# A shorter way to the first scores, a seventh shared PSUM bank and a new plan for the opening of an attention and MLP kernel

## The chip, the core and the metric

The kernel runs on one core of one Trainium2 chip. A time is the device time of one execution in microseconds (us), and a quoted median is over the runs of one job on one chip. The span that a profile shows is some 1.8 us shorter than the time of the same execution. "Slow" means over 1.5% above the fastest run of the same kernel, and comparisons use the other runs.

The engines are TensorE (PE, its weight loads PEld), VectorE (DVE), ScalarE (ACT), GpSimd (POOL) and SyncE (SP). In this kernel POOL issues the loads. SP issues stores, the DMA transposes and the copies of the attention mask ("mask rows").

## The reference, cut to what matters

Block-sparse attention over 4 batches, 8 heads, 768 tokens and head size 64, followed by a residual MLP: a product over the tokens ("token mixing"), then two feed-forward layers of 512 to 2048 to 512.

```python
scores = scale * np.matmul(q, k.transpose(0, 1, 3, 2))
# mask: neighbouring blocks, first and last blocks, three sampled blocks for each query block
scores = np.where(mask, scores, -1000000000.0)
# ... softmax, times v, heads put side by side: x ...
a1 = alpha1 * x + beta1
tok = np.einsum('ts,bsd->btd', w_tok, a1)
u = x + lam * tok
a2 = alpha2 * u + beta2
ch = np.maximum(a2 @ w_ch1, 0.0) @ w_ch2
return (u + lam * ch).astype(np.float32)
```

The kernel works on 16 pairs of heads. The first six pairs take their mask out of the score product ("single scores"). The later ones are multiplied with a mask tile after the exponential ("paired scores").

## The kernel before: the parts that matter

**The order is a plan made ahead.** Every piece of work is a `Job` with an assumed duration, a priority, what it waits for, and the buffers that it takes and gives back. A list scheduler on the host walks through assumed time. Whenever an engine is free it emits the ready job of the best priority, and where TensorE would idle it emits dummy products (`fill`). The result is a fixed instruction order for every engine. `T0` is the assumed time at which the engines are free behind the hand-written opening.

```python
    T0 = 6600.0
    free_at = dict(NEVER=1e9, NONE=0.0, PE=T0, ACT=T0, DVE=T0, POOL=4800.0, SP=T0)
    slots = dict(
        **{b: 1 for b in BANKS}, cp=1, ops=1, eT=NET, head=NQB, vext=NV, ld=NLD, rel=3,
        # ...
    )
```

All loads of q, k and v go through one ring of `NLD = 6` buffers, and they are issued by one queue in a fixed order. A buffer comes free when VectorE has cast its content into another tile:

```python
        putv[p] = Job("DVE", dve(768, 4, 155), (2 if p == 0 else 3, p, 2), pv_put, [ld[p, "v2"]],
                      take=("vext",), give=("ld",))
```

**PSUM.** Six banks are one tile, `ps6`. The second layer adds up in two tiles of its own, `cp` and `ops`. Since `ps6` is one tile, `bank_order` replaces the ordinary ordering by a finer one: it puts waits only between accesses of the same bank. An earlier access of `ps6` stays a reason to wait if the two instructions also share another tile by name:

```python
        for n in names:                      # the other tiles of this instruction
            for r in shared.get(n, ()):      # earlier ps6 instructions that name the same tile
                if r.engine != ins.engine or ins.engine != mybir.EngineType.PE:
                    real[r.name] = r
            shared.setdefault(n, []).append(ins)
        tc.declare_no_dep(ins, group=psum, keep=list(real.values()), reason="other banks")
```

The first layer's evictions (the copies out of PSUM) write the hidden tile `hts` (16 blocks of 384 columns), block `f` by block `f`, out of `ps6`. The second layer's products read four blocks of `hts` at a time.

**The opening.** Nine wide warm products keep TensorE busy until the first operands are there:

```python
    keep_warm(9, 512)
    # ...
    first_cast(0)
    block_mask()          # ends in a subtraction and multiplication on VectorE
    flatA = transposes(rel0, 0, "b0", range(0, 3))
    flatB = transposes(rel0, 0, "b1", range(3, 6))
    for w in range(2):    # mask product, out of kx[0]
        nc.tensor.matmul(t[0:NBLK, 0:HS], mbb[MB, :], kx[0][MB, ts(w, HS)], start=True, stop=True)
    # ... four copies and two casts out of PSUM ...
    keep_warm(7, P)
```

The softmax here doesn't subtract the row's maximum and nothing guards it: scores larger than these inputs give would overflow.

## Time and profile before

| | before |
|---|---|
| time, median of 3 runs | 310.68 us (310.44 to 310.88) |
| span of the profiled execution | 308.2 us |
| first score product starts | 7.72 us |
| last single exponential starts | 67.9 us |
| first paired scores start | 69.9 us |
| dummy products after 8 us, busy time | 6.85 us |
| ScalarE's waits for single scores, 8 to 62 us | 2.4 us |
| second-layer weight loads issued | 38.4 to 43.3 us |

TensorE is busy from one end to the other, so the time can fall only where it is busy with dummies or waits for the opening.

### The profile page before, as it was taken

What the parts mean: (1) busy time and instruction counts of PE and PEld (TensorE: products, weight loads), DVE (VectorE), ACT (ScalarE), POOL (GpSimd) and SP (SyncE); (2) the same over time, 40 slices, a digit from 0 to 9 for tenths busy, and PEclk for the clock granted to TensorE, in tenths of its full rate; (3) what the DMA queues carried; (4) which work ended last, traced back from release to release, by engine and by line L of the source; (5) the groups of instructions that cost most, each with busy time, mean ns of one, the idle gap of its engine ahead of it and who ended that gap; (6) DMA issues with size and microseconds to landing.
All of it is one profiled execution on the core that took longest, in us unless ns stands there. A gap on an engine that the chain in (4) does not pass through costs nothing.

```text
span 308.2 us, 7605 instructions
## 1 busy us (share of the span) xinstructions
PE 302.7 (98%) x3197; PEld 189.0 (61%) x3197; DVE 207.6 (67%) x434; ACT 206.3 (67%) x272; POOL 53.2 (17%) x91
## 2 busy tenths in 40 slices
PE   7999999999999999999999999999999999999995
PEld 3687788775656557555656557555656665555444
DVE  3699898879979788778759788778768730010111
ACT  4999998988676667577676666577658727428000
POOL 4656532001121121212021121120000000000000
PEclk9999999999999999999999999999999999999999
DMA  6999999993347634874444624983110110010121
GB/s 150 186 258 224 212 203 215 177 146 68 51 101 123 104 62 54 146 121 95 76 93 84 102 62 56 147 107 79 28 37 34 28 28 34 34 70 0 50 89 68
DMA packets 47210, 30.81 MB, mean 100 GB/s; under 512 B 27552, under 2 KB 43080, under 8 KB 47176
## 3 DMA queue, kind: packets, MB, share of 16 engines
q0 software_dynamic: 15984, 15.47, 32.0%
q1 hardware_dynamic: 30940, 14.61, 21.0%
q8 instruction: 25, 0.41, 0.6%
q10 hardware_dynamic: 252, 0.24, 0.2%
q14 instruction: 9, 0.07, 0.1%
HBM read 32.04 MB, written 6.33 MB: 124 GB/s over the span
## 4 chain that ended last, share of the span: by engine, by line
PE 76%; DMA 15%; issue 4%; POOL 3%; DVE 1%; POOLq 0%
PE ps L1026 26%; PE cp L1076 22%; DMA v<-in_v_dram 9%; PE ops L870 8%; PE ps L837 8%; PE ps L947 7%; PE ops L1076 5%; DMA k<-in_k_dram 3%; DMA wtk<-in_moe_w_tok_dram 3%; DMA q2f<-in_q_dram 1%; POOL q L383 1%; POOL k L383 1%; POOL w1b L448 1%; POOL v L383 0%; DVE x_sb L957 0%
## 5 line engine op out<-in xcount | busy, mean ns | idle before, releaser
L789 ACT ACTIVATE eT<-ps 128x1024 f16<-128x1024 f32 x90 | 87.0, 1023 | 29.4 <-PE ps L837 28.6
L1026 PE MATMUL ps<-uT,w1b 128*128 128x384 bf16 (+1 forms) x512 | 92.9, 326 | 0.1
L1039 ACT ACTIVATE hts<-ps,b1t 128x384 bf16<-128x384 f32 x106 | 61.4, 583 | 40.3 <-PE ps L1026 36.4
L1076 PE MATMUL cp<-w2b,hts 128*128 128x512 bf16 (+1 forms) x320 | 77.2, 374 | 0.0
L794 DVE TENSOR_TENSOR eT<-eT,maskT 128x1024 f16<-128x1024 f16 x90 | 60.6, 686 | 12.7 <-ACT eT L789 12.5
L1026 PEld LDWEIGHTS <-w1b 128*128 128x128 bf16 x512 | 46.9, 98 | 30.3 <-ACT eT L789 1.0
L1076 PEld LDWEIGHTS <-hts 128*128 128x128 bf16 x400 | 36.6, 98 | 36.4 <-issue 3.0
L731 ACT ACTIVATE eT<-ps 128x1024 f16<-128x1024 f32 (+1 forms) x55 | 52.4, 1020 | 3.4 <-PE ps L716 3.2
L870 PEld LDWEIGHTS <-eT 128*128 128x128 f16 x720 | 30.9, 97 | 15.7 <-issue 3.8
L947 PE MATMUL ps<-a1p,wtokT 128*128 128x128 bf16 x576 | 36.2, 219 | 0.0
L870 PE MATMUL ops<-vext,eT 128*128 128x65 f16 x720 | 35.8, 193 | 0.0
L947 PEld LDWEIGHTS <-wtokT 128*128 128x128 bf16 x576 | 32.9, 98 | 1.5 <-issue 0.6
L1093 DVE TENSOR_TENSOR ot<-x_sb,cp 128x512 f32<-128x512 f32 (+1 forms) x20 | 13.5, 673 | 28.4 <-PE cp L1076 28.3
L716 PE MATMUL ps<-qx,kx 88*128 88x512 bf16 (+1 forms) x144 | 31.7, 326 | 0.7 <-ACT qx L303 0.7
L381 POOL COPY held<-flag 1x1 bf16<-1x1 bf16 x24 | 10.5, 438 | 123.1 <-DVE flag L401 123.1
L837 PE MATMUL ps<-qx,kx 64*128 64x512 bf16 (+1 forms) x240 | 26.1, 326 | 0.0
L756 PEld LDWEIGHTS <-eT 128*128 128x128 f16 x432 | 18.2, 97 | 4.6 <-DVE x_sb L691 0.6
L756 PE MATMUL ops<-vext,eT 128*128 128x65 f16 x432 | 20.2, 193 | 0.0
L957 DVE TENSOR_TENSOR x_sb<-x_sb,ps 128x384 f32<-128x384 f32 x32 | 17.6, 550 | 3.5 <-PE ps L947 3.1
L691 DVE TENSOR_TENSOR x_sb<-ops,rcp 128x384 f32<-128x384 f32 x32 | 17.8, 558 | 1.1
L1093 DVE TENSOR_TENSOR ot<-x_sb,ops 128x512 f32<-128x512 f32 (+1 forms) x5 | 3.2, 635 | 22.5 <-PE ops L1076 22.5
L1043 DVE TENSOR_SCALAR hts<-ps,b1t 128x384 bf16<-128x384 f32 x22 | 13.6, 618 | 6.8 <-PE ps L1026 5.2
(69 smaller groups left out, 227.2 us busy)
## 6 DMA issues: line engine op xcount, KB each, us to landing
out_dram<-ot SPq DMA_DIRECT2D x23, 256.0 KB
v<-in_v_dram POOLq DMA_DIRECT2D x16, 192.0 KB, 4.4
q<-in_q_dram POOLq DMA_DIRECT2D x15, 192.0 KB, 4.7
k<-in_k_dram POOLq DMA_DIRECT2D x15, 192.0 KB, 3.5
w1b<-in_moe_w_ch_dram POOLq DMA_DIRECT2D x4, 512.0 KB, 9.9
w2b<-in_moe_w_ch_dram POOLq DMA_DIRECT2D x4, 512.0 KB, 15.0
wtk<-in_moe_w_tok_dram POOLq DMA_DIRECT2D x3, 384.0 KB, 9.6
maskT<-mask_rows SPq DMA_DIRECT2D x14, 72.0 KB
```

Of the source, the lines that this page charges most:

```text
L691: nc.vector.tensor_tensor(out=x_sb[:, s0 : s0 + NT, h * D : (h + 1) * D], in0=op[:, :, 0:D], in1=rcp[:].unsqueeze(2).broadcast_to([P, NT, D]),
L716: nc.tensor.matmul(sps[:, f - u * UN : f - u * UN + w], kx[h][0:KC, ts(jt, P)], qx[h][0:KC, c : c + w], start=True, stop=True,)
L731: nc.scalar.activation(eT[:, c], sps[:, c], AF.Exp, bias=EXPB, scale=SCALE)
L756: nc.tensor.matmul(ops[p, a][:, t * VW : t * VW + D + 1], eTs[p, u][:, ts(i - u * GU, P)], vx[:, a, jt, 0 : D + 1], start=(i % HT == 0), s ...
L789: nc.scalar.activation(eT[:], sps[:], AF.Exp, bias=EXPB, scale=SCALE)
L794: nc.vector.tensor_tensor(out=e, in0=e, in1=maskT[:, u, :].unsqueeze(1).broadcast_to([P, 2, 512]), op=ALU.min,)
L837: nc.tensor.matmul(sps[:, a * 512 + lo : a * 512 + lo + w], kx[sl][r, ts(jt, P)], qx[sl][r, c : c + w], start=True, stop=True,)
L870: nc.tensor.matmul(ops[p, a][:, t * VW : t * VW + D + 1], eTs[p, u][:, a * 512 + c * P : a * 512 + (c + 1) * P], vx[:, a, jt, 0 : D + 1], ...
L947: nc.tensor.matmul(tp[:, j, :], wtokT[:, s, ts(3 * g + j, P)], tl["a1p", p][:, s, :], start=(s == 0), stop=(s == NT - 1),)
L1026: nc.tensor.matmul(hp[:, 0:nc_], w1b[:, dk, ts(f, P)], uTs[b][:, dk, hf * HS : hf * HS + nc_], start=(dk == 0), stop=(dk == 3),)
L1039: nc.scalar.activation(hts[kk][:, f, :], hp[:, 0:HS], AF.Relu, bias=b1t[:, f : f + 1], scale=1.0)
L1076: nc.tensor.matmul(cps[kk, mi][:, 0:w], hts[kk][:, nk, ts(m, P)], w2tile[0][:, nk, lo : lo + w], start=(nk == 0), stop=(nk == 15),)
```

## The change

The intent is to bring the first scores earlier and use the time saved: one load for two small tables, the mask product out of `kx[3]` so that a copy need not wait for it, the mask arithmetic moved into the evictions, and a shorter warm stretch. Beyond that, the bank `cp` becomes bank `b6` of `ps6`, so that single products may use it until the second layer starts. Three of the first batch's four transposes go to DMA (`UTN`), token mixing of a batch's last pair goes ahead (`PR`, `TOKP`), `LEAD` (how far the plan lets the scores run ahead of the feed-forward layers) becomes 17, and the planner starts at 5.6 us. The core of the diff:

```diff
-LEAD = 18
+LEADS = (17, 17, 17, 17, 17, 17, 17, 17, 17, 17, 17, 17, 17, 17, 17, 17)
+PR = 0
+UTN = 3
+TOKP = 1
+T0 = 5600.0                     # was 6600.0
...
-    ps6 = ps.tile([P, 6 * 512], FP, name="ps6", tag="ps6", bufs=1)
+    ps6 = ps.tile([P, 7 * 512], FP, name="ps6", tag="ps6", bufs=1)
+    ALL = BANKS + ("b6",)
...
-    keep_warm(9, 512)
+    keep_warm(7, 512)
+    keep_warm(2, P)
...
-            t[0:NBLK, 0:HS], mbb[MB, :], kx[0][MB, ts(w, HS)], start=True, stop=True
+            t[0:NBLK, 0:HS], mbm[MB, :], kx[3][MB, ts(w, HS)], start=True, stop=True
...
+    nc.scalar.activation(
+        qx[0][MB, HS:S], bqs[1][0:NBLK, 0:HS], AF.Identity, bias=-BIG, scale=BIG
+    )
...
-        if b == 0:
+        if b == 0 and n >= UTN:
...
-                take = ((("cp", "ops") + (BANKS if kk == 2 * B - 1 else ()), ("cpsel", kk, mi)),) if r == 0 else ()
+                take = ((("b6", "ops") + (BANKS if kk == 2 * B - 1 else ()), ("cpsel", kk, mi)),) if r == 0 else ()
...
-                        opts = BANKS[:2]
+                        opts = BANKS[:2] if st["ch"] else ("b0", "b1", "b6")
```

## The prediction

> **What bounds the kernel now.** I read the page's busy table and its forty slices first, then the order of time of the first 20 us, then the waits, then the windows of the first 80 us.
>
> ```profile
> PE 302.7 (98%) x3197; PEld 189.0 (61%) x3197; DVE 207.6 (67%) x434; ACT 206.3 (67%) x272; POOL 53.2 (17%) x91
> ...
> PE   7999999999999999999999999999999999999995
> ...
> ACT  4999998988676667577676666577658727428000
> ...
> DMA  6999999993347634874444624983110110010121
> ```
> TensorE (PE) is busy from the second slice to the last; ScalarE (ACT) is full only in the first eight slices, to about 62 us, and the DMA engines are full in the same stretch.
>
> Busy PE is not useful PE, so I counted the work. One product of N columns costs N/2.4 GHz plus about 2.7 ns: the trace's stretch of 64 products of 384 columns takes 10.40 us in the chain, 162.5 ns each. First feed-forward layer 512 x 162.7 ns = 83.3 us; second, 368 x 216 plus 32 x 109 = 83.0; token mixing 576 x 56 = 32.3; transposes 132 x 56 = 7.4; value products 1152 x 30.3 = 34.9; single scores 54 x 0.433 = 23.4; paired scores 90 x 0.25 = 22.5. The sum is 286.8 us. The span is 308.2: 7.7 before the first score, some 3.5 behind the last product, and so about 10 us of lost PE time in between. That is all that the later parts of the change can win.
>
> Where those 10 us lie, the waits and the order of time show:
>
> ```profile
> 7.07 0.55 DVE L302 CAST qx<-ps 24x384 bf16<-24x384 f32 x1
> 7.21 0.47 ACT L303 CAST qx<-ops 24x384 bf16<-24x384 f32 x1
> 7.72 1.03 PE L716 MATMUL ps<-qx,kx 88*128 88x512 bf16 x5 [0.66 <-ACT qx L303]
> 8.14 12.31 ACT L731 ACTIVATE eT<-ps 128x512 f16<-128x512 f32 x14 [0.46 <-PE ps L716]
> ```
> The columns are start, length, engine, line. The first score starts at 7.72 us, right after two casts of the mask, and from then on ACT runs exponentials without a gap. The first six head pairs are ACT's stretch: 54 exponentials of 1.02 us, ending at 68.97. PE's real work is too short to fill it, so the kernel puts in dummy products on the warm tile; after 8 us they keep PE some 4.7 us (starts of one group to the next), and none comes after 60 us. Behind 70 us real products stand back to back and lose only 0.02 to 0.04 us in each us inside the groups of products.
>
> **What the Trainium skill says.** "TensorE: Matmul & The Clock Gate", section "What's actually happening": the array starts at half clock and is released after about 3.4 us of sustained work. The trace agrees: the nine first warm products take 427 ns each from 1.19 us, the transposes at 5.01 still go at 107 ns, the products from 6.5 us are fast. So two shorter warm products are affordable, because the array stays busy. "ScalarE: Activation LUTs", "Table sets": identity is in every table set. The trace has one table load, at 2.60 us; the new identity activation should bring no second one. "DMA: Bandwidth & Descriptors", "Issuing engines are not separate DMA queues": all queues share the same 16 engines. The trace agrees: loads that land in 3.3 us at 75 us take 15.0 us at 53, where the windows put the DMA share over 1. "PSUM", "Specifications": eight banks; six shared ones, one for the second layer (cp) and one for the outputs (ops) are all of them, so the seventh bank is cp renamed, not new room.
>
> **The change part by part.**
>
> *Way to the first scores.* Before, warm products hold PE until 5.01 although both casts were done at 4.40 and the weight load of the first transpose started at 4.58. Seven wide and two narrow ones end at 1.19 + 7 x 0.427 + 2 x 0.107 = 4.39, so the transposes come 0.3 to 0.4 us earlier, ending at about 5.5. The copy of kx at 6.31 then waited for the mask product, only because both touch kx0:
>
> ```profile
> DVE kx L298 <- PE ps L294: 1.2, 1, 1.2
> ```
> With the block pattern read from kx3, that copy starts with the transposes' end, some 0.8 us earlier. The subtraction before the mask product (0.38 us on DVE) goes; it moves into the two evictions, which were there anyway. Then DVE has 0.36 + 0.35 + 0.55 = 1.26 us and ACT 3 x 0.47 = 1.41 us from about 5.5, and the first score comes at about 6.95: 0.75 us earlier. Fusing two small tables into one DMA saves an issue of 0.3 us, but the mask chain (ready at 5.11, used at 5.79) was not last. ACT is gap-free behind it, so I count the 0.75 in full.
>
> *Transposes of the first batch.* For three of its four pairs the PE transposes and copies give way to DMA transposes. That takes 18 products of 56 ns off PE, 1.0 us, and two ACT copies of 0.80 and one DVE copy of 0.56. ACT's stretch gets 1.6 us shorter; PE has 1.0 us less to do in it. At most 0.6 more of dummy work goes.
>
> *Seventh bank, priorities, lead of 17.* The single products before the first layer had two banks, now three; token mixing of each batch's last pair and the VectorE work around it go ahead. The dummies at 57.5 us (0.6) and some at 26 to 31 us (1.3) stand where nothing else could go. I grant 0.3 to 1 us of them. Behind 70 us the order changes, the work doesn't.
>
> Sum: 0.75 + 1.0 + about 1.0 = 2.75 us, if the DMA transposes cost nothing.
>
> **The rivals.**
> 1. *The DMA transposes come late.* The SP queue that issues them is taken by the mask rows:
>
> ```profile
> 46.47 15.78 SPq L556 DMA_DIRECT2D maskT<-mask_rows  x18
> 62.55 1.32 SPq L657 DMA_TRANSPOSE qx<-rel  x1
> 63.98 1.81 SPq L657 DMA_TRANSPOSE kx<-rel  x1
> ```
> The second and third pairs' inputs are ready at 45.6 and 50.3 us, so one or both may queue behind the mask, to 62 us, and then land at some 65. The first layer began at 59.7 and did six groups of 0.65 us, 3.9 us, before 69. Without them ACT's stretch ends earlier too (two evictions of 0.73), but 1 to 2 us of dummy or empty PE time appear, and the transposes for pair six start 2.4 us later. Against it: the schedule is a static plan, and whoever set this surely ordered for it. I take 0.5 us off for it on average, so 2.25 remain.
> 2. *ACT stays the bound but at other places.* Then the 0.75 and the 1.6 us of copies are won on ACT, and PE's 1.0 is eaten by dummies: the time falls by 1.5 to 2.3 us, much the same.
> 3. *The early gain is given back.* PE after 70 us is saturated, and an earlier start only lets it start its work earlier; this is not lost unless loads are late. The loads of pairs one and two land at 10 to 13 us, and ACT had no gap there; if ACT runs 0.75 us ahead, it may meet a wait for the second pair's data (dummies at 8.9 to 12.9 show PE waiting). Then 0.3 to 0.7 is lost again and the whole is about 1.5.
> 4. *A large gain.* Over 2% is 6.2 us, which would need nearly all lost PE time and the start; nothing here does it.
>
> **Range and chances.** 310.68 less 2.25 is 308.4. If all goes well, 3 us or a bit more and perhaps some luck of the new order: 306.2. If the late transposes and a wait at 10 us take all, 310.6. A gain over 2% (below 304.5) I give 0.04; a loss over 2% (above 316.9) 0.01.
>
> **What would show it.** The first score in the order of time: right at 6.7 to 7.1 us, wrong if above 7.4. The copy L298's successor must no longer wait for the mask product. One table load. Dummies after 8 us at 3 to 4.5 us against 4.7. The uT transposes: right if all three lie before 57 us, rival 1 if SP issues any behind the mask rows and the first group of the first layer starts after 62 us. Last single exponential: at about 66.5 us if ACT's savings hold, against 68.97. Stretches after 80 us should be as before, shifted. What would make it wrong: a late SP transpose that starves PE, or a re-ordered middle part that loses or wins more than 1 us by itself.

## More of the kernel before

The load queue of this kernel, of which the prediction does not speak, reads as follows in the order of time (columns: start, length, engine, line, output<-input, count, idle time before and what ended it):

```profile
35.92 0.71 POOL L383 DMA_DIRECT2D v<-in_v_dram  x1 [0.44 <-DVE lam_bcb L516]
38.36 0.76 POOL L456 DMA_DIRECT2D w2b<-in_moe_w_ch_dram  x1 [1.73 <-PE ps L947]
...
42.55 0.74 POOL L456 DMA_DIRECT2D w2b<-in_moe_w_ch_dram  x1 [0.29 <-DMA k<-in_k_dram]
51.35 0.70 POOL L383 DMA_DIRECT2D q<-in_q_dram  x1 [8.06 <-DVE rel L571]
```

The four weight loads go out between 38 and 43 us. The queue then waits 8 us for a buffer, with the large loads already under way.

## The result, and the profile after

The changed kernel takes 321.25 us (320.44 to 321.9, four runs), the kernel before 310.78 in the same job. The ratio is 1.0337 with a 95% interval of 1.0306 to 1.0367. It is 3.4% slower, outside the predicted range on the far side. A ratio here is the mean time of one kernel's fast runs over that of the other's of the same rounds, so it is not quite the ratio of the medians.

| | before | after |
|---|---|---|
| first score product | 7.72 | 6.91 us |
| dummy products after 8 us, busy | 6.85 | 9.85 us |
| ScalarE's waits for single scores, 8 to 62 us | 2.4 | 4.4 us |
| last single exponential starts | 67.9 | 70.0 us |
| first paired scores | 69.9 | 85.9 us |
| PE busy in 70 to 80 us | 10.00 | 5.02 us |

The page after, whose rows answer to those that the prediction shows:

```profile
PE 305.4 (96%) x3190; PEld 189.4 (59%) x3190; DVE 207.0 (65%) x433; ACT 204.6 (64%) x269; POOL 53.1 (17%) x91
...
PE   7999999994899999999999999999999999999995
...
ACT  4999699882487756976657666866767534618100
...
PEclk9999999999799999999999999999999999999999
DMA  6999996999519454545647563537021011020021
```

A hole has come up in PE's tenth slice (72 to 80 us) and in ScalarE's at the same place. In the slices before it the DMA row stays high until 80 us, where the row of before falls to 3 at 69. That hole is 5 us of TensorE's time. It has a second price: PEclk, the clock granted to TensorE, falls to 7 in the slice behind it. The clock records of the trace have half clock from 80.04 to 83.45 us, so the 3.1 us of products after the hole took about 1.5 us longer than at full clock (an estimate from these times). The rest of the loss is nowhere to be seen at this resolution.

The opening itself did what it was meant to. In the order of time of the changed kernel:

```profile
5.22 0.36 DVE L302 COPY kx<-ps 64x384 bf16<-64x384 bf16 x1 [0.29 <-PE ps L288]
...
5.88 0.48 ACT L305 ACTIVATE qx<-ops 24x384 bf16<-24x384 f32 x1
...
6.91 1.02 PE L723 MATMUL ps<-qx,kx 88*128 88x512 bf16 x5 [0.65 <-ACT kx L312]
```

The copy of `kx` now waits for the transposes (L288) and no longer for the mask product. The first score starts 0.81 us earlier. There is one table load, at 2.19 us.

The load queue of the changed kernel, in the order of time:

```profile
37.88 0.72 POOL L393 DMA_DIRECT2D k<-in_k_dram  x1
50.45 0.72 POOL L393 DMA_DIRECT2D v<-in_v_dram  x1 [11.85 <-DVE uT L1014]
51.16 3.04 POOL L466 DMA_DIRECT2D w2b<-in_moe_w_ch_dram  x4
54.19 0.71 POOL L393 DMA_DIRECT2D q<-in_q_dram  x1
```

The queue stands still for 11.85 us waiting for a buffer. All six buffers are then held by loads whose casts have not run. In the kernel before, the cast of pair four's v at 34.99 us freed a buffer for the load of pair six's v, issued at 35.92; here that cast comes at 52.03 us, and the load has to take the buffer that the cast of pair five's q frees at 50.15. (Which load takes which buffer was read from the built programs.) The four large weight loads go out at 51 to 54 us instead of 38 to 43. There they meet the mask rows, which SP issues from 51.22 us for 17.6 us. The q of pair seven, issued at 54.19, lands at 76.9 us, 22.7 us later; q loads of the kernel before in the same stretch took 8.4 (median). What that does to VectorE and TensorE:

```profile
76.90 0.36 DVE L578 COPY rel<-q 128x768 bf16<-128x768 bf16 x1 [5.81 <-DMA q<-in_q_dram]
...
79.66 0.62 DVE L1051 TENSOR_SCALAR hts<-ps,b1t 128x384 bf16<-128x384 f32 x1
...
80.34 2.76 PE L1034 MATMUL ps<-uT,w1b 128*128 128x385 bf16 x8 [5.32 <-DVE hts L1051]
```

VectorE waits 5.81 us for q. The eviction of a first-layer bank (L1051) stands behind that in VectorE's order, and TensorE waits 5.32 us for the bank. VectorE kept to its program order here: TensorE's last group before the wait had ended at 75.0 us, so the eviction's bank had been full for over 4 us, and still the eviction started only at 79.66, behind the copy and the work that follows it.

### The profile page after: what moved, and what is told of

The parts are those of the page before. It is cut to its first block, busy times and chain, and to the rows that moved or that the text cites. A ratio compares the mean times of both kernels' runs of the same rounds, so it can differ in the third digit from the quotient of the medians.

```text
span 318.9 us, 7605 instructions
## 1 busy us (share of the span) xinstructions
PE 305.4 (96%) x3190; PEld 189.4 (59%) x3190; DVE 207.0 (65%) x433; ACT 204.6 (64%) x269; POOL 53.1 (17%) x91
## 4 chain that ended last, share of the span: by engine, by line
PE 74%; DMA 13%; issue 6%; ACT 3%; POOL 1%; DVE 1%; SPq 0%; POOLq 0%; ACTq 0%
PE ps L1034 23%; PE ps L1084 22%; PE ops L877 7%; DMA k<-in_k_dram 7%; PE ps L955 7%; PE ps L844 7%; PE ops L1084 5%; DMA v<-in_v_dram 3%; DMA q<-in_q_dram 2%; PE ps L723 2%; ACT eT L796 2%; ACT hts L1047 1%; DMA identb<-ident_c 1%; PE ops L763 1%; PE ps L246 1%
## 5 line engine op out<-in xcount | busy, mean ns | idle before, releaser
L1034 PE MATMUL ps<-uT,w1b 128*128 128x384 bf16 (+1 forms) x512 | 94.3, 329 | 5.3 <-DVE hts L1051 5.3
L1047 ACT ACTIVATE hts<-ps,b1t 128x384 bf16<-128x384 f32 x103 | 59.4, 582 | 47.1 <-PE ps L1034 35.7
L1084 PE MATMUL ps<-w2b,hts 128*128 128x512 bf16 (+1 forms) x320 | 77.1, 375 | 1.1 <-ACT hts L1047 1.1
L1084 PEld LDWEIGHTS <-hts 128*128 128x128 bf16 x400 | 36.8, 98 | 38.2 <-issue 4.4
L877 PEld LDWEIGHTS <-eT 128*128 128x128 f16 x720 | 30.7, 97 | 14.6 <-issue 2.8
L877 PE MATMUL ops<-vext,eT 128*128 128x65 f16 x720 | 35.5, 193 | 0.0
L1101 DVE TENSOR_TENSOR ot<-x_sb,ps 128x512 f32<-128x512 f32 (+1 forms) x20 | 13.4, 670 | 27.6 <-PE ps L1084 27.5
L763 PEld LDWEIGHTS <-eT 128*128 128x128 f16 x432 | 17.6, 97 | 4.7 <-ACT eT L738 0.6
L1051 DVE TENSOR_SCALAR hts<-ps,b1t 128x384 bf16<-128x384 f32 x25 | 15.4, 615 | 7.6 <-PE ps L1034 7.1
L965 DVE TENSOR_TENSOR x_sb<-x_sb,ps 128x384 f32<-128x384 f32 x32 | 17.6, 549 | 4.0 <-PE ps L955 3.7
L763 PE MATMUL ops<-vext,eT 128*128 128x65 f16 x432 | 18.9, 193 | 0.2 <-ACT eT L738 0.2
L844 PEld LDWEIGHTS <-kx 64*128 64x128 bf16 x240 | 9.3, 94 | 15.2 <-issue 5.0
```

Source lines behind the costliest of these rows:

```text
L763: nc.tensor.matmul(ops[p, a][:, t * VW : t * VW + D + 1], eTs[p, u][:, ts(i - u * GU, P)], vx[:, a, jt, 0 : D + 1], start=(i % HT == 0), s ...
L844: nc.tensor.matmul(sps[:, a * 512 + lo : a * 512 + lo + w], kx[sl][r, ts(jt, P)], qx[sl][r, c : c + w], start=True, stop=True,)
L877: nc.tensor.matmul(ops[p, a][:, t * VW : t * VW + D + 1], eTs[p, u][:, a * 512 + c * P : a * 512 + (c + 1) * P], vx[:, a, jt, 0 : D + 1], ...
L1034: nc.tensor.matmul(hp[:, 0:nc_], w1b[:, dk, ts(f, P)], uTs[b][:, dk, hf * HS : hf * HS + nc_], start=(dk == 0), stop=(dk == 3),)
L1047: nc.scalar.activation(hts[kk][:, f, :], hp[:, 0:HS], AF.Relu, bias=b1t[:, f : f + 1], scale=1.0)
L1084: nc.tensor.matmul(cps[kk, mi][:, 0:w], hts[kk][:, nk, ts(m, P)], w2tile[0][:, nk, lo : lo + w], start=(nk == 0), stop=(nk == 15),)
```

## The experiments

Where the expectations speak of theories by letter, A is that the earlier planner start and the re-planned first 60 us are the loss, and B that the DMA transposes behind the mask rows are. Edits called "+ub" add one dependency, without which the scheduler can order two halves of one job wrongly; s3 does not build without it. The edit is not neutral. Built again afterwards, the changed kernel differs with it at 16 of the 6381 places in TensorE's order (weight loads and products), but s4, s16 and s18, which build without it, differ from about the 1270th of some 6400 places on, so these three measure a plan that "+ub" moved too.

```diff
-            ubs.append(Job("DVE", 555.0, (pr, p, g), ubm, [jx, l_a2], take=("ub",) if g == 0 else ()))
+            ubs.append(Job("DVE", 555.0, (pr, p, g), ubm, [jx, l_a2] + ubs[:1], take=("ub",) if g == 0 else ()))
```

All runs gave correct results.

### Single parts undone or done (four runs, one chip; before 311.1 us)

**s1**: the changed kernel with everything that re-plans taken back; left are the opening and the seven-bank code (+ub).

```diff
-LEADS = (17, ...)
-PR = 0
-UTN = 3
-TOKP = 1
-T0 = 5600.0
+LEADS = (18,) * 16
+PR = 2
+UTN = 0
+TOKP = 3
+T0 = 6600.0
```

> The changed kernel with its opening (one table, mask pattern from kx3, fewer warm products) and its seven-bank code, but with the old start time T0 of the plan (6600), the old priorities and lead, and PE transposes for the first batch: the planner then orders the rest as the kernel before does. Theory A (the moved plan is the loss) and theory B (the DMA transposes are the loss) both expect a gain of the opening alone: the first score at about 6.9 us, the whole 0.5 to 0.9 us shorter than before, 309.8 to 310.3 us. Theory C (the new opening itself loses, for instance by a colder PE) expects 312 us or more.

Measured: 317.45 us (316.06 to 319.58), ratio 1.0205 [1.0146, 1.0263]. With the planned order of before and an opening that is faster in the trace, 6 us are lost. So the re-planning alone is not the whole cause.

**s2**: the kernel before with the planner start alone.

```diff
-    T0 = 6600.0
+    T0 = 5600.0
```

> The kernel before with nothing changed but the planner's start time T0, 5600 instead of 6600. Theory A: the planned order of VectorE and of the load queue changes, the cast of the value block of pair 4 comes some 16 us later, the load queue stands still some 10 us before 51 us, and the time rises by 4 us or more, to 315 to 322 us. Theories B (DMA transposes) and D (third bank) expect no change, 310.8 plus or minus 1 us.

Measured: 318.18 us (317.26 to 318.8), ratio 1.022 [1.0176, 1.0264]. This one number costs 7 us and shows the hole of the changed kernel by itself. Its load queue:

```profile
46.80 0.72 POOL L383 DMA_DIRECT2D k<-in_k_dram  x1 [13.34 <-DVE rel L571]
52.30 0.72 POOL L383 DMA_DIRECT2D v<-in_v_dram  x1 [4.79 <-DVE uT L1006]
53.02 3.06 POOL L456 DMA_DIRECT2D w2b<-in_moe_w_ch_dram  x4
```

The weight loads again go out at 53 us, and PE waits 3.6 us for an eviction at 62.8. So there are at least two causes that do not need each other.

**s3** and **s4**: the changed kernel with only the planner start, or only the DMA transposes, taken back (+ub each).

```diff
-T0 = 5600.0
+T0 = 6600.0        # s3
-UTN = 3
+UTN = 0            # s4
```

> The changed kernel whole, with T0 back at 6600. Theory A: the load queue stands still less than 5 us around 40 to 50 us, and the time is 309 to 314 us; the third DMA transpose may still queue behind the mask rows (first layer from about 65 us), which is why it may stay above the kernel before. Theory B: the DMA transposes are kept, so the time stays at 318 us or more.

> The changed kernel with PE transposes and copies for all four pairs of the first batch, as before (T0 stays 5600, three banks, new priorities). Theory A: the load queue still stands still for some 10 us before 49 us and the time stays at 316 to 322 us. Theory B: without the DMA transposes the time falls to 309 to 312 us.

Measured: s3 327.24 us, ratio 1.0515 [1.0466, 1.0564]; s4 327.63 us, ratio 1.0544 [1.048, 1.0609]. Both are slower than the changed kernel. In s3 two of the DMA transposes come behind the mask rows, at 67.67 us, which is rival 1 of the prediction, here in full; in s4 the load queue waits 10.1 us in two waits for one kind of cast. TensorE's longest wait is for VectorE in both (3.9 and 3.6 us, for the same operation). Theory B finds no support in its plain form, for taking the transposes away made it slower. But the main thing to learn is about the method: each knob makes the scheduler re-order everything, so a part undone alone measures a new plan and not the part. The next two experiments leave the plan alone.

### The opening alone and the bank alone, on the kernel before (before 311.07 us)

**s5**: the opening's edits alone, with `cp` as its own tile, planner start 6.6 us. **s6**: `cp` as bank `b6`, and nothing else. The instruction order is exactly that of before.

```diff
-    ps6 = ps.tile([P, 6 * 512], FP, name="ps6", tag="ps6", bufs=1)
-    wps = ps.tile([P, 512], FP, name="cp", tag="cp", bufs=1)
+    ps6 = ps.tile([P, 7 * 512], FP, name="ps6", tag="ps6", bufs=1)
+    ALL = BANKS + ("b6",)      # and "cp" -> "b6" wherever it is named
```

> The kernel before with the new opening alone (one table, mask pattern from kx3, subtraction moved into the evictions, seven wide and two narrow warm products); cp keeps its own PSUM tile, T0 and every planned order as before. Theory E (the run with opening and seven banks was slow because a start 0.8 us ahead of the plan makes the load queue meet other waits, so that loads land later): 313 us or more. Theory F (it was slow because the second layer's bank lies in the shared PSUM tile, where the ordering rule keeps waits between accesses that share any other tile): 309.5 to 310.5 us.

> The kernel before with the second layer's bank (cp) made the seventh bank of the shared PSUM tile, nothing else; the planned order is that of before. Theory F: evictions of the first layer wait for second-layer products of the same hidden tile, PE loses some us between 70 and 250 us, and the time rises to 312 to 317 us. Theory E: no change, 310.3 to 311.3 us.

Measured: s5 311.12 us, ratio 0.9978 [0.9906, 1.005], so no gain of the opening can be seen. The interval is too wide to exclude the 0.75 us that I predicted. s6 316.95 us (fast runs 315.5 to 317.46), ratio of the fast runs 1.0159 [1.0079, 1.0238]. A pure renaming of a bank costs about 5 us. Comparing the two built programs, the order of every engine is the same but the waits are not: they differ on 7 of ScalarE's and 6 of VectorE's instructions and on some of TensorE's. First-layer evictions of both engines wait for second-layer products, and second-layer products wait for later evictions. The reason is the exception in `bank_order`: the second layer's products now write to `ps6`, they share `hts` with the evictions by name, and the rule keeps every such pair, whether or not the two touch the same columns of `hts`.

### The rule mended, and a seventh load buffer (four runs, one chip; before 310.68 us)

The mend records the columns of `hts` that each instruction touches, and drops a kept pair of TensorE and another engine whose columns don't overlap:

```diff
                 if ap.tensor.name != psum:
                     names.add(ap.tensor.name)
+                    if not ap.tensor.name.startswith("hts"):
+                        continue
+                    # lo, hi: the columns; kept in span[ins.name, ap.tensor.name]
...
+                if n.startswith("hts") and r.engine != ins.engine and mybir.EngineType.PE in (r.engine, ins.engine):
+                    x, y = span[ins.name, n], span[r.name, n]
+                    if x[0] > y[1] or y[0] > x[1]:
+                        continue
                 if r.engine != ins.engine or ins.engine != mybir.EngineType.PE:
                     real[r.name] = r
```

s9 is s6 with the mend, s8 the changed kernel with it, s11 is s8 with `NLD = 7`, and s13 the changed kernel with `NLD = 7` and the old rule.

> The changed kernel with one thing mended: the ordering rule keeps a wait between a PE product and an eviction over the hidden tile only where the columns they touch overlap. Theory F (needless waits are part of the loss, the moved plan the rest): PE no longer loses 0.2 to 0.8 us in each 50 us between 100 and 250 us; the stall at 74 to 80 us stays; the time falls from 321 to 314 to 318 us. If the waits were all of it: 309 to 311. If they are nothing: 320 to 322.

> The kernel before with the second layer's bank in the shared tile (316.4 us on fast runs) and the ordering rule mended in the same way; its waits are then those of the kernel before. Theory F: 310.3 to 311.5 us. If the place of the bank itself cost the time, not the waits: 315 us or more.

> The changed kernel with the mended rule and seven load buffers instead of six. Theory A2 (the rest of the loss is the load queue, which waits near 12 us for the one buffer that the late value cast of pair 4 holds): the wait at 38 to 50 us goes, the second-layer weights are asked for before 45 us, the q block of pair 7 lands before 68 us instead of at 76.9, PE has no stall at 75 to 80 us, and the time is 309 to 312 us. Rival: the mask rows and the first-batch DMA transposes still push the q and k transposes of pair 6 to 70 us, and the time stays at 314 us or more.

> The changed kernel with seven load buffers and the old ordering rule. If the two causes stand side by side, this gains what the buffer gains, and keeps the waits: 314 to 317 us. If the stall hides the waits (not additive), 316 to 319.

| run | rule | buffers | us | ratio to before |
|---|---|---|---|---|
| changed kernel (its own job) | old | 6 | 321.25 | 1.0337 |
| s13 | old | 7 | 318.75 | 1.0236 [1.0165, 1.0307] |
| s8 | mended | 6 | 316.93 | 1.0193 [1.0116, 1.027] |
| s11 | mended | 7 | 313.89 | 1.0083 [0.9997, 1.017] |
| s9 (bank alone) | mended | 6 | 310.93 | 0.9997 [0.992, 1.0074] |

s9 settles the bank: with the waits gone (all those of ScalarE and VectorE are again the ones of before), and nothing else different, s6's 5 us are gone. The cleanest pair on the changed kernel is s13 and s11, on one chip, different only in the rule: 4.86 us. ScalarE's waits from 70 to 310 us (columns: waiting engine, tile and line, what it waited for, us in total, times, longest), first with the old rule:

```profile
ACT hts L1047 <- PE ps L1034: 33.5, 24, 8.8
ACT eT L796 <- PE ps L844: 27.4, 28, 2.6
ACT hts L1047 <- PE ps L1084: 10.5, 7, 2.9
```

then with the mended one:

```profile
ACT hts L1059 <- PE ps L1046: 38.6, 29, 8.8
ACT eT L808 <- PE ps L856: 28.7, 31, 2.6
```

The third row is the fault. An eviction of the first layer (`hts<-ps`) waits for second-layer products (L1084), seven times and 10.5 us in total. No data asks for it. With the mended rule the row is gone, and those waits are back with the products that fill the bank. TensorE's busy time from 100 to 250 us, its windows in stretches of 50, goes from 145.65 to 148.05 us of 150. The changed kernel's own trace has that row at 6.4 us, five times; the kernel before has none.

The second step is the load buffer: s8 to s11 3.0 us, the changed kernel to s13 some 3 us by the ratios (1.0337 to 1.0236). The load queue of s11:

```profile
38.20 0.72 POOL L405 DMA_DIRECT2D v<-in_v_dram  x1
39.25 0.76 POOL L478 DMA_DIRECT2D w2b<-in_moe_w_ch_dram  x1 [0.33 <-issue]
...
44.91 0.74 POOL L478 DMA_DIRECT2D w2b<-in_moe_w_ch_dram  x1 [0.71 <-DMA k<-in_k_dram]
```

The stop of 11.85 us is gone, the weight loads lie at 39 to 45 us as before, and the hole has filled. It was 5 us deep, with the half clock behind it, and filling it is worth 3. Part of the difference is visible: in s11 PE loses 0.8 us of the stretch from 60 to 70 us instead, where the changed kernel lost nothing. The windows from 70 to 80 us (stretch, length, then busy us and count for PE, PEld, DVE, ACT and POOL, then clock, DMA share and GB/s) of the changed kernel and of s11:

```profile
70.00:80.00 10.00, 5.02 (x61) 3.19 (x57) 3.75 (x10) 3.13 (x7) 0.00 (x0) 1.00 1.27 127
```

```profile
70.00:80.00 10.00, 9.95 (x96) 5.88 (x94) 7.43 (x18) 5.78 (x14) 0.89 (x2) 1.00 0.81 128
```

### What is left of the loss: four runs on one chip (before 311.09 us)

About 2.6 us of s11 were open. s14 is s11 with everything that re-plans taken back, as in s1; s16 takes back the DMA transposes alone, s17 priorities and lead alone; s18 is s14 with the planner start at 5.6 us.

```diff
 NLD = 7                        # all four, with the mended rule
+T0 = 6600.0; UTN = 0; PR = 2; TOKP = 3; LEADS = (18,) * 16    # s14 (+ub)
+UTN = 0                                                       # s16 (+ub)
+PR = 2; TOKP = 3; LEADS = (18,) * 16                          # s17 (+ub)
+UTN = 0; PR = 2; TOKP = 3; LEADS = (18,) * 16                 # s18 (+ub)
```

> The changed kernel with the mended ordering rule and seven load buffers, and with every part that re-plans the work undone: planner start 6.6 us, no DMA transposes for the first batch, old priorities, lead of 18. Left of the change are the short opening and the seventh bank. Theory (needless waits and the re-planned first 60 us are all of the loss): 309.5 to 311.5, ratio 0.995 to 1.003, the second-layer weight loads issued before 45 us, PE without a stall at 60 to 80. Rival (the seventh bank or the opening costs something by itself beside the waits): 313 or more. If a seventh load buffer also takes away the odd slow executions, all single times lie below 312.

> The run with the mended rule and seven load buffers (313.89) with the DMA transposes of the first batch undone. If the DMA transposes and the mask rows behind them on the SP queue hold the remaining 3 us: 310.5 to 312, the first transposes of pair six before 67 us. If the order of VectorE's early work (planner start, priorities) holds them: 313 or more.

> The run with the mended rule and seven load buffers (313.89) with the old priorities for token mixing and a lead of 18; DMA transposes and planner start stay as changed. If the priorities hold the remaining 3 us: 310.5 to 312. If it is the DMA transposes or the planner start: 313 to 315.

> The plain kernel of this series (mended rule, seven load buffers, everything that re-plans undone) with one thing put back: the planner start at 5.6 us. With six buffers and the old rule this one number cost 7 us on the kernel before. If the held load buffer was the way in which it cost: 310 to 312 here, no wait of 10 us on the POOL queue between 36 and 51 us. If the earlier start costs by other reordering: 314 or more.

Measured: s14 312.25 us, ratio 1.003 [0.9997, 1.0063]; s16 314.33, 1.0109 [1.0061, 1.0157]; s17 313.38, 1.0085 [1.0044, 1.0126]; s18 314.76, 1.0086 [1.0023, 1.0149]. Neither the transposes nor the priorities alone hold the rest. Read by itself, s18 says that the planner start does. By the medians it costs 2.5 us over s14 (1.7 by the ratios, and the intervals overlap). Its load queue still waits 7.1 us, and 7.9 us in two more waits, though PE does not stall in it.

The traces showed a cause that I had not looked for. s5 and s18 have the first scores in 1.86 and 1.87 us, where the kernel before takes 1.03. TensorE in s5, in the order of time:

```profile
4.95 0.82 PE L275 MATMUL ps<-identb,rel 128*128 128x128 bf16 x6 [0.38 <-ACT rel L268]
...
7.58 1.86 PE L712 MATMUL ps<-qx,kx 88*128 88x512 bf16 x5 [0.21 <-ACT kx L299]
9.24 0.85 PE L275 MATMUL ps<-identb,rel 128*128 128x128 bf16 x6
...
11.74 1.06 PE L234 MATMUL cp<-warm 128*128 128x512 bf16 x2
```

Six transposes of the second pair take 0.85 us here and 0.50 in the kernel before (at 8.59 us); products run at half speed until 13.8 us. The Trainium skill, "TensorE: Matmul & The Clock Gate", "What's actually happening", says that the clock is released after one busy window of about 3.4 us, and that the window is free-running, "it doesn't reset when your kernel starts". The warm stretch of before lasts from 1.19 to past 5 us and the transposes follow without a gap. The shortened one ends at 4.57, 3.38 us after its start, and the operands come between 4.57 and 4.95 us, so there is a gap of 0 to 0.4 us.

The packed traces hold records of the clock, from the release on, and these show both the window and the chance. Between two changes of the clock lies a whole multiple of 3.413 us: in the changed kernel 75.09, 3.41 and 235.52 us, which are 22, 1 and 69 windows. Of the 12 profiled executions with the short stretch, six were released at 4.83 to 5.75 us. The other six (s3, s5, s8, s14, s16, s18) were released only at 10.64 to 13.85 us; counted back from there in steps of 3.413 us, they too had a window that ended at 6.26 to 7.23 us, and it did not release them. All eight executions with the long stretch, counting the runs below, were released at 4.92 to 7.08 us, four of them in a window that ended after 6 us. So a window that ends later than some 6 us finds too little work with the short stretch and enough with the long one, and where the windows lie changes from execution to execution. How much work a window needs is not shown. The gap alone does not decide: it was 0.23 us in the changed kernel and s13, which were released early, and 0.05 in s18, which was not.

### The long warm stretch put back (before 311.12 us; the last run 311.3)

s19 is s14, s20 is s18, s21 is s11, and s23 is s5, each with this edit:

```diff
-    keep_warm(7, 512)
-    keep_warm(2, P)
+    keep_warm(9, 512)
```

> The plain kernel (short opening, seventh bank, mended rule, seven load buffers, everything that re-plans undone; 312.25) with the nine wide warm products back, as in the kernel before. Its profiled execution had TensorE at half clock until 13.2 us: five first scores in 1.87 us, six transposes of the second pair in 0.85, where the kernel before has 1.03 and 0.50, and ScalarE lost 5.1 us to waits for scores against 2.4. Theory (the shorter warm stretch leaves the release of the clock to chance): first scores in 1.03 us, waits of ScalarE at 2 to 3 us, 309.5 to 311, all single times within 1.5 us of each other. Rival (the half clock is an accident of the profile and costs the timed runs nothing): 312 or more, as without them.

> The same kernel with the planner start at 5.6 us and nine wide warm products (314.76 with the short warm stretch). If what the early start still cost there was the half clock that its profiled execution also had: 310 to 311.5. If the early start costs by its own plan (more dummy products after 8 us: 9.0 us busy against 6.4): 312.5 to 314.5.

> The changed kernel with the mended rule and seven load buffers (313.89) and nine wide warm products. If waits, load buffer and clock are all of the loss: 310.5 to 312. If the early planner start holds the rest: 313 to 314.5, with dummy products after 8 us again at 8 us or more against 6.9 of the kernel before.

> The kernel before with the opening alone (one table, mask pattern from its own tile, mask arithmetic in the evictions), but with the nine wide warm products of before. If the first scores' way is worth its gain when the clock is released in time: first score at 7.0 to 7.4 us, five scores in 1.03 us, and 310.0 to 310.8, ratio 0.996 to 1.000. If the early gain is given back at once whatever the clock: 311 and ratio 1.000 or above. Executions that stall at 60 to 80 us, as some of the kernel before do, would show as 313 to 315 with a clock below 0.996.

| run | short stretch: ratio | long stretch: us | ratio |
|---|---|---|---|
| s18, s20 | 1.0086 | 311.99 (311.3 to 312.32) | 1.0008 [0.9971, 1.0045] |
| s11, s21 | 1.0083 | 313.22 (312.37 to 314.15) | 1.0044 [1.0002, 1.0085] |
| s14, s19 | 1.003 | 313.98 (310.37 to 315.22, two of six slow) | 1.003 [0.9972, 1.0088] |
| s5, s23 | 0.9978 | 311.37 (310.0 to 313.82) | 1.0022 [0.9981, 1.0063] |

In all four profiles the first scores take 1.02 to 1.03 us. TensorE in s23, in the order of time:

```profile
7.42 1.02 PE L711 MATMUL ps<-qx,kx 88*128 88x512 bf16 x5 [0.65 <-ACT kx L298]
8.28 0.50 PE L274 MATMUL ps<-identb,rel 128*128 128x128 bf16 x6
```

Only the first pair shows a gain in the time: 2.8 us by the medians, 2.4 by the ratios, just outside the noise, and the jobs ran on different chips. The pairs of s14 and s5 show none, though their short versions were at half clock in their profiles too. So the half clock is shown in the traces, and what it costs at the end is shown by one pair of four. That pair also takes back what s18 seemed to say. With seven buffers, the mended rule and the long warm stretch, no cost of the early planner start can be seen (0.3 us, with an interval up to 1.4). s11 to s21 points the same way (0.7 us by the medians) but is within the spread. s19 missed what I expected: four of its six runs are at 313.85 to 315.22 us with mean clocks of 0.988 to 0.995, two at 310.37 and 312.12 with clock 1.0. Executions of the kernel before do this too (three of eleven in that job, 313.4 to 313.6 us at clocks of 0.993 to 0.995). s9's profiled execution, at 313.33 us, was of this kind, and TensorE loses its time there between 60 and 80 us, waiting for VectorE. Its clock records have half clock for one window, 71.93 to 75.35 us, after TensorE had idled for 1.91 us. A window of half clock takes 0.0055 off the mean clock of a 310 us execution, so the listed clocks probably count such stalls: one at 0.993 to 0.995, as in all four runs of the changed kernel, two at 0.988 (the first release is not in this mean, as the records start with it). I take the stall for the same late loads of pairs six and seven, in a milder form, but no run separates it. s23 shows 310.0 to 313.82, with two of its six runs of that kind.

No version that beats both kernels came out. The best (s5, s9, s20 and s23) equal the kernel before.

## Why the prediction was wrong

The loss can be laid out as one ladder of ratios, each step an edit of the changed kernel; a ratio of 0.001 is 0.31 us:

| step | ratio | worth |
|---|---|---|
| changed kernel | 1.0337 | |
| mended rule (s8) | 1.0193 | 4.5 us |
| seventh load buffer (s11) | 1.0083 | 3.4 us |
| long warm stretch (s21) | 1.0044 | 1.2 us |
| transposes, priorities and lead undone (s20) | 1.0008 | 1.1 us |

The first two steps are confirmed by a second pair each (s13 to s11, changed kernel to s13). The last two are each smaller than the intervals of their runs, so their sizes are not firm; firm is that no loss can be told from the noise at s20 (interval up to 1.4 us), which keeps the opening but for its warm stretch, the seventh bank and the early planner start.

- **The opening: right in the trace, wrong in what it is worth.** I predicted the first score at 6.95 us (measured 6.91), the copy freed from the mask product (so it was) and one table load (one). That 6.91 lies so near is partly luck: the 12 executions with this opening show 6.75 to 7.58 us, by when the operands came and the clock was released. "I count the 0.75 in full" is not borne out: the opening alone gives a ratio of 0.9978 with the short and 1.0022 with the long warm stretch, and by the medians both equal the kernel before (311.12 to 311.07 and 311.37 to 311.3 us). The intervals reach 2 us, so a gain of some tenths is not excluded. In the changed kernel ScalarE's waits for single scores rose from 2.4 to 4.4 us in the same stretch. With the long stretch alone they stayed at 2.4 (s23) and still no gain showed at the end; whether those 0.3 us of earlier start were lost or only lie within the noise is open.
- **"So two shorter warm products are affordable, because the array stays busy": failed.** It does not stay busy enough: half of the profiled executions with the short stretch ran at half clock until 10.64 to 13.85 us. The changed kernel's own profile was not among them (released at 4.95), so no trace shows that its 3.4% contain this.
- **Transposes of the first batch: the mechanism held, the gain did not.** All three DMA transposes lay before 57 us (36.49 and 49.90 us), as I required. The last single exponential started at 70.0 us and not 66.5, and dummies rose to 9.85 us, where I had said they would shrink. The dummies count differs from my 4.7 because that was taken from starts of groups; by busy time it was 6.85 before.
- **Seventh bank: the failed step that cost most.** I wrote "the seventh bank is cp renamed, not new room" and gave the third bank a gain of 0.3 to 1 us. That was true of the room, and it left out the waits. The renaming moved the second layer under the kernel's own ordering rule, and the needless waits cost 4.5 to 4.9 us. I had read the diff for what the bank can hold, not for what is decided by the tile's name.
- **"Behind 70 us the order changes, the work doesn't": failed.** The work is the same, but the plan puts a cast of a value block so late that its load buffer holds up the load queue for 11.85 us. The hole at 75 to 80 us costs 3.0 to 3.4 us, as the seventh buffer shows.
- **The rivals.** Rival 1 (transposes late behind the mask rows) came true for pair six, at 69.56 us against 62.55, and in full in s3, but does not explain the loss: without the DMA transposes the changed kernel was slower still (s4), and s11 gained nothing (s16), though both runs have a new plan. Rival 3 (early gain given back, "not lost unless loads are late") was the right heading, with the wrong loads and far too small a size (I had allowed 0.3 to 0.7 us). I set 0.01 on a loss of over 2%, because I looked only for gains that could fail and asked of nothing whether it could add a wait.

## What to carry to other kernels

When a buffer is moved into a tile that has its own ordering rule, compare the waits of the two built programs before anything else: with the order unchanged, every wait that is new is a cost to be explained. In a kernel whose order is a plan made ahead, a change of one assumed time re-orders every queue, so test parts with the plan held fixed, and read first where the queue of loads stands still. A warm stretch that is just as long as the operands usually take leaves the clock to chance; look at several executions before calling it long enough. A stall of TensorE can cost more than its length: read the clock behind it.

## What the Trainium skill lacked or had wrong

- "TensorE: Matmul & The Clock Gate", "What's actually happening", gives the release after one busy window and the chance in its phase, and the traces agree with both. It does not say how much work makes a window busy: with 3.38 us of warm products, windows that ended at 6.26 to 7.23 us did not release the clock (six executions), and with nine wide products windows that ended at 6.05 to 7.08 us did (four).
- The same page, "Seeing it yourself", says that profiles hold the clock's transitions and warns that they are not to be fully trusted. Here the records agree with the durations where they were compared: in s5 the release is recorded at 13.85 us and products take twice as long until about then, and in the changed kernel half clock is recorded from 80.04 to 83.45 us. What misleads is the view: before the first record its clock column reads 1.00, as in s5 from 9.2 to 13.4 us, and only the durations show the half clock.
- No page speaks of ordering within one PSUM tile that holds several banks: here a rule that went by tile names cost 4.5 to 4.9 us without a byte more or less to move.
